# Float64 weights in a planned kernel: a 16-bit copy, a masked shift and one combining pass in place of three VectorE passes

## The chip, the cores and the metric

The kernel runs on one core of a Trainium2 chip. The metric is the device time of one execution in microseconds (us), from its start to its end on that core. The profile covers one such execution. Its span is a little shorter than the execution's time, because launch and completion lie outside it.

## The reference

Four sequences of 768 positions go through windowed attention with 8 heads of 64, and then through a gated feed-forward block. The weights `moe_w_in` (512 x 1024) and `moe_w_out` (512 x 512) reach the kernel as float64, because they are scaled by a float64 number; `moe_w_sg` (768 x 768) is float32.

```python
scores = scale * np.matmul(q, k.transpose(0, 1, 3, 2)) + bias[None, :, :, :]
scores = np.where(keep, scores, -1000000000.0)        # 8 global keys, 96 local ones
a = np.exp(scores - np.max(scores, axis=-1, keepdims=True))
a = a / (np.sum(a, axis=-1, keepdims=True) + 1e-09)
attn = np.matmul(a, v).astype(np.float32)             # then laid out as x [B, S, 512]
...
h = gelu(x @ w_in)
u, v = (h[..., :d_ff // 2], h[..., d_ff // 2:])
v_n = (v - mu) / np.sqrt(var + 1e-06) * g_ln
v_s = np.einsum('ts,bsd->btd', w_sg, v_n) + b_sg[None, :, None]
return (x + (u * v_s) @ w_out).astype(np.float32)
```

## The kernel before

**Attention.** The work is cut into 48 units: a batch, a pair of heads and 256 query rows. Each unit loads its q and k (`qk`) and its `v`, multiplies scores on TensorE (`s_ps`, line 915), adds the bias and takes the row extreme on VectorE (line 937), exponentiates on ScalarE (line 942), adds a tiny number to the sums (`pst`, line 951) and takes their reciprocal (line 955). For the first 16 units the probabilities are turned on TensorE (`tps<-diag,p`, line 1040) against a diagonal matrix that holds the reciprocals (`diag`, line 973, on VectorE or GpSimd). From unit 16 on they are scaled in place (lines 961 and 963) and turned through VectorE and DRAM (`tt`, `far`, `pt`). Then they multiply `v` (`av`, line 1070).

**Feed-forward.** Every fp32 product is made of three matmuls on a high and a low part (lines 577 to 579 in `Moe.terms`; `win`, `wsg` and `wout` hold both parts of the weights). For each batch there are six products of the normalised half (`win,x`), eight of the gate's half (`x,win`), eight of the sequence mix (`wsg,z`) and eight of the output (`gt,wout`). They are laid among the attention units of the next batch.

**Weights.** `load_split` brings one chunk of a weight matrix in: 4 chunks of 512 columns of `w_in` first (the normalised half, staged in the places called z), then 8 of 256 columns (the gate's half, places gt), then 8 of 256 columns of `w_out` (places t and diag). These 20 are float64, so a chunk arrives as pairs of 32-bit words, `raw`, the low word first. ScalarE multiplies the high word, read as a float32, by 2^-112 into `f` (line 742). Three VectorE passes follow: shift `f` left by 3 (line 745), OR in the low word's top three bits (line 747), OR in the high word's sign (line 749). After that `f` is an fp32 number; it is rounded to the high part (752 on ScalarE or 753 on VectorE), and the rest becomes the low part (754 on GpSimd or VectorE). Chunks of `w_sg` need only these last two.

**What sets the order.** A planner (`Plan`) gets every operation with its possible engines, each with a time that the code states (`on_act`, `on_dve`, `on_pool` and so on), and its reads and writes. It draws 200 plans from a fixed seed, each with its own random shifts of the due times, replays each, and keeps the best. The instructions are issued in that order, and each engine runs its own in that order. In gaps that the planner foresees on TensorE in the first 29 us, `keep_on` puts matmuls that multiply zeros (line 526, called fillers here) so that the engine isn't idle there; their results are overwritten.

Of the kernel before, what the change touches and what calls it, by code (L numbers as in the profile page):

```python
# [13 lines left out]
F32R = mybir.dt.float32r  # L14
BF16 = mybir.dt.bfloat16
I32 = mybir.dt.int32
AF = mybir.ActivationFunctionType
ALU = mybir.AluOpType
PSUM = bass.MemoryType.PSUM
# [101 lines left out]
def on_act(n, more=0.0):  # L121

    return "ACT", 0.055 + n / 1200 + more, 0.165 + n / 1200 + more


def on_dve(n, more=0.0):
    return "DVE", 0.065 + n / 960 + more, 0.155 + n / 960 + more


def on_dve_sb(n, more=0.0):  # L130

    return "DVE_SB", 0.065 + n / 960 + more, 0.155 + n / 960 + more


def on_pool(n, more=0.0):
    return "POOL", 0.05 + n / 390 + more, 0.08 + n / 390 + more


def on_pool_ts(n, more=0.0):

    return "POOL_TS", 0.05 + n / 390 + more, 0.08 + n / 390 + more
# [36 lines left out]
def parts(used):  # L178

    return [(b.buf, b.part) if isinstance(b, View) else b if isinstance(b, tuple) else (b, None)  # L180
            for b in used]
# [35 lines left out]
class Now:  # L217
# [5 lines left out]
    def op(self, ways, reads=(), writes=()):  # L223
        for b, _ in parts(writes):
            if b.kind and b.tile is None:
                n = self.next[b.kind] = self.next.get(b.kind, -1) + 1
                b.slot = n % self.places[b.kind]
        ways[0][-1]()
# [325 lines left out]
class Moe:  # L554
# [38 lines left out]
    def gelu2(self, out, h, n):  # L593

        nc, op = self.nc, self.plan.op
        op([on_act(n) + (lambda: nc.scalar.activation(
            out.ap, h.ap, AF.Square, scale=math.sqrt(GELU_C * GELU_A)),)], [h], [out])
        op([on_dve(n) + (lambda: nc.vector.scalar_tensor_tensor(
            out.ap, out.ap, GELU_C, h.ap, ALU.add, ALU.mult),)], [h], [out])
        op([on_act(n, 0.05) + (lambda: nc.scalar.activation(out.ap, out.ap, AF.Tanh),)], [], [out])  # L600
        op([on_dve(n) + (lambda: nc.vector.scalar_tensor_tensor(
# [125 lines left out]
def load_split(nc, plan, stage, t, src, k, cols, part):  # L727


    n, op = cols.stop - cols.start, plan.op  # L730
    rows = slice(k * P, (k + 1) * P)
    wire = lambda words: ("SP", 0.38, P * words * 4 / RATE)
    raw, f = stage(n)
    if src.dtype != mybir.dt.int64:
        op([wire(n) + (lambda: nc.sync.dma_start(f.ap, src[rows, cols]),)], [], [f])
    else:
        words = lambda: raw.ap.bitcast(I32).rearrange("p (n w) -> p n w", w=2)
        a = lambda: f.ap.bitcast(I32)
        op([wire(2 * n) + (lambda: nc.sync.dma_start(
            raw.ap.bitcast(I32), src.bitcast(I32)[rows, 2 * cols.start:2 * cols.stop]),)], [], [raw, f])  # L740

        op([on_act(n, 0.07) + (lambda: nc.scalar.mul(
            f.ap, words()[:, :, 1].bitcast(F32), 2.0 ** -112),)], [raw], [f])

        op([("DVE_SB", 0.07 + n / 1850, 0.15 + n / 1850, lambda: nc.vector.tensor_scalar(
            a(), a(), 3, None, ALU.logical_shift_left))], [], [f])
        op([on_dve_sb(n, 0.02) + (lambda: nc.vector.scalar_tensor_tensor(  # L747
            a(), words()[:, :, 0], 29, a(), ALU.logical_shift_right, ALU.bitwise_or),)], [raw], [f])
        op([on_dve_sb(n, 0.02) + (lambda: nc.vector.scalar_tensor_tensor(  # L749
            a(), words()[:, :, 1], -0x80000000, a(), ALU.bitwise_and, ALU.bitwise_or),)],  # L750
           [raw], [f])
    op([on_act(n, 0.03) + (lambda: nc.scalar.copy(t[:, 0, k, cols], f.ap),),
        on_dve_sb(n / 2) + (lambda: nc.vector.tensor_copy(t[:, 0, k, cols], f.ap),)], [f], [(t, part)])
    lo = lambda eng: eng.tensor_tensor(t[:, 1, k, cols], f.ap, t[:, 0, k, cols].bitcast(F32),  # L754
                                       ALU.subtract)
    op([on_pool(n) + (lambda: lo(nc.gpsimd),), on_dve_sb(n) + (lambda: lo(nc.vector),)],
       [f], [(t, part)])


def local_global_attention_moe(tc, qk_in, v_in, q_t, k_t, v_n, n_gl, w_in, g_ln, w_sg_t, b_sg,  # L760
# [11 lines left out]

    nc.scalar.activation(small[:, 1:2], w.mhalf, AF.Exp)

# [21 lines left out]

    ni = cp.tile([P, 4], I32, name="ni")
    nc.sync.dma_start(ni, n_gl.bitcast(I32).rearrange("(o n) -> o n", o=1).to_broadcast([P, 4]))

# [125 lines left out]
    def softmax(n):  # L925
# [4 lines left out]
        for i in range(2):  # L930
            own = u == 0 and i == 0
            for g in range(2):
# [9 lines left out]
                op([on_act(nk, 0.225) + (lambda p=p, g=g, nk=nk, i=i: nc.scalar.activation(  # L942
                    p[:, g, 0:nk], p[:, g, 0:nk], AF.Exp, bias=st[:, 0, i, g:g + 1], scale=-1.0,
                    accum_out=st[:, 1, i, g:g + 1]),)], [], [(p, g), (st, (i, g))])

        def sums(a):
            return st.ap.rearrange("p a i g -> p a (i g)")[:, a]

        op([on_act(4, 0.13) + (lambda: nc.scalar.activation(
            sums(1), sums(1), AF.Identity, bias=w.tiny),),  # L950
            ("POOL_TS", 0.24, 0.28, lambda: nc.gpsimd.tensor_scalar(  # L951
# [316 lines left out]
    def phase(ns, items, prep=()):  # L1268

        total = sum(c for c, _ in items)  # L1270
        items, prep, done = list(items), list(prep), 0

        def upto(part):
            nonlocal done
            while items and done + items[0][0] / 2 <= part * total:
                c, f = items.pop(0)
                done += c
                f()

        n_prep, todo = len(prep), []  # L1280
        while len(ns) and (todo[-1][-1] if todo else ns[0] - 1) < ns[-1]:
            todo.append(group(todo[-1][-1] + 1 if todo else ns[0]))
        for a, group_ns in enumerate(todo):
            step(group_ns)
            while prep and n_prep - len(prep) < (a + 1) * n_prep / len(todo):
                load_split(nc, plan, *prep.pop(0))
            upto((a + 1) / len(todo))
        upto(2)
# [33 lines left out]
    for b in range(B + 1):  # L1322
# [30 lines left out]
        if b == 1:  # L1353
            general = cp.tile([P, 1], I32, name="general")
            op([("DVE", 0.9, 1.0, find_general)], [xs[b, 0, 0]], [])
# [11 lines left out]
def dense_path(tc, future, ng, nl, iota, w, qkv, out):  # L1367
    nc = tc.nc
    q_t, k_t, v_n = qkv
    with ExitStack() as ctx:  # L1370
# [20 lines left out]
        with tc.For_i(0, B, 1) as b:  # L1391
            x = []
            for j in range(NPAIR):
# [10 lines left out]
                for i in range(NT):  # L1404
# [6 lines left out]
                    for h in range(2):  # L1411
# [16 lines left out]
                        nc.vector.tensor_scalar(s, s, st[:, 0:1], None, ALU.subtract)  # L1428
                        nc.scalar.activation(s, s, AF.Exp, accum_out=st[:, 1:2])
                        nc.vector.tensor_scalar(st[:, 1:2], st[:, 1:2], 1e-9, None, ALU.add)  # L1430
# [79 lines left out]
```

## Time and profile before

| | |
|---|---|
| Time, median of 3 runs | 417.9 us (415.46 to 419.92) |
| Profiled execution | 416.7 us |
| Its span | 414.8 us |
| TensorE busy | 402.6 us (97%) |
| VectorE busy | 309.8 us (75%) |
| ScalarE busy | 223.1 us (54%) |
| GpSimd busy | 202.6 us (49%) |

In rows of the profile PE is TensorE, DVE is VectorE, ACT is ScalarE, POOL is GpSimd and SP is the queue that issues the DMAs; `L749` is line 749 of the kernel. A row such as `stage<-stage 128x256` names the tile that is written, the tiles that are read, and the shape; the staging tiles of the weights, `raw` and `f` alike, are called `stage`. "Idle before" is the time for which the engine stood still ahead of an instruction, and the name behind it is what ended that time. "Issue" means that the engine waited for nothing that the profile shows.

### The profile page before, as it was taken

The numbers are of one execution on the slowest core, as the hardware profiler recorded it, in microseconds if no ns is written. First come the engines' busy times: TensorE is split into PE (matmuls) and PEld (weight loads), VectorE is DVE, ScalarE is ACT, GpSimd is POOL, SyncE is SP. The second block draws the span as 40 slices with busy tenths as digits, with TensorE's granted clock in tenths as the row PEclk, the third lists the DMA queues.
The fourth block names the chain that finished last, engine by engine and source line by source line (L and its number), as shares of the span: only waits on it lengthen the run. The fifth ranks groups of instructions, "written<-read, shape, count | busy, mean of one in ns | idle before, by whom it ended". The sixth has DMA issues, their size and how long they took to land.

```text
span 414.8 us, 12362 instructions
## 1 busy us (share of the span) xinstructions
PE 402.6 (97%) x4579; PEld 363.2 (88%) x4580; DVE 309.8 (75%) x1014; ACT 223.1 (54%) x731; POOL 202.6 (49%) x340
## 2 busy tenths in 40 slices
PE   8899989999999999999999999999999999999994
PEld 5677767899998888999999888999999888999994
DVE  6898889999977888966666798956767568743362
ACT  5988997966747565654155665644245234311220
POOL 2324546677868666654455277354355342323200
PEclk9999999999999999999999999999999999999998
DMA  7856583438889686754697685645777501001002
GB/s 234 298 170 202 185 269 107 141 131 241 256 263 299 203 252 202 207 141 135 191 295 222 188 276 145 193 107 160 218 227 205 171 33 40 0 2 57 21 2 81
DMA packets 50034, 70.21 MB, mean 169 GB/s; under 512 B 5808, under 2 KB 33968, under 8 KB 49968
## 3 DMA queue, kind: packets, MB, share of 16 engines
q1 hardware_dynamic: 49968, 69.36, 55.7%
q8 instruction: 38, 0.62, 0.6%
q14 instruction: 28, 0.23, 0.2%
HBM read 50.99 MB, written 18.35 MB: 167 GB/s over the span
## 4 chain that ended last, share of the span: by engine, by line
PE 86%; DVE 4%; ACT 3%; DMA 2%; issue 2%; POOL 1%; SPq 1%; POOLq 0%; DVEq 0%; ACTq 0%
PE mm_ps L577 24%; PE mm_ps L579 22%; PE mm_ps L578 22%; PE av L1070 7%; PE s_ps L915 7%; PE tps L1040 2%; ACT p L942 2%; DMA pt<-far 1%; DMA stage<-in_w_in_dram 1%; PE s_ps L526 1%; DVE p L937 1%; DVE stage L747 1%; DVE stage L749 1%; SPq L1013 1%; POOL z L615 0%
## 5 line engine op out<-in xcount | busy, mean ns | idle before, releaser
L942 ACT ACTIVATE p<-p,pst 128x192 f32<-128x192 f32 (+1 forms) x192 | 84.2, 443 | 43.4 <-DVE pst L937 43.2
L577 PE MATMUL mm_ps<-wsg,z 128*128 128x384 f32 x192 | 64.7, 337 | 0.0
L579 PE MATMUL mm_ps<-wsg,z 128*128 128x384 f32 x192 | 64.3, 335 | 0.2 <-POOL z L615 0.2
L578 PE MATMUL mm_ps<-wsg,z 128*128 128x384 f32 x192 | 64.2, 334 | 0.0
L963 POOL TENSOR_SCALAR p<-p,pst 128x192 f32<-128x192 f32 (+1 forms) x124 | 56.7, 473 | 14.0 <-DVE pst L955 11.1
L937 DVE CUSTOM_DVE_ANT_0 p<-s_ps,bias 128x192 f32<-128x192 f32 (+1 forms) x192 | 56.6, 339 | 5.7 <-PE s_ps L915 5.5
L1070 PE MATMUL av<-pt,v 64*64 64x128 f32 (+1 forms) x1408 | 48.1, 250 | 2.5 <-issue 1.8
L1070 PEld LDWEIGHTS av<-pt,v 64*64 64x64 f32 x1408 | 40.9, 133 | 10.7 <-issue 6.7
L703 POOL TENSOR_TENSOR o<-o,x 128x384 f32<-128x384 f32 x28 | 28.4, 1013 | 38.3 <-DVE o L700 27.7
L577 PE MATMUL mm_ps<-x,win 128*128 128x384 f32 x128 | 44.1, 344 | 0.0
L915 PE MATMUL s_ps<-qk 64*64 64x192 f32 (+1 forms) x768 | 41.9, 323 | 1.7 <-issue 1.7
L579 PE MATMUL mm_ps<-x,win 128*128 128x384 f32 x128 | 42.9, 335 | 0.6 <-POOL win L754 0.6
L577 PE MATMUL mm_ps<-gt,wout 128*128 128x384 f32 x128 | 43.0, 336 | 0.0
L579 PE MATMUL mm_ps<-gt,wout 128*128 128x384 f32 x128 | 43.0, 336 | 0.0
L578 PE MATMUL mm_ps<-gt,wout 128*128 128x384 f32 x128 | 42.8, 335 | 0.0
L578 PE MATMUL mm_ps<-x,win 128*128 128x384 f32 x128 | 42.8, 334 | 0.0
L577 PE MATMUL mm_ps<-win,x 128*128 128x512 f32 x96 | 40.0, 417 | 0.0
L1005 DVE STREAM_TRANSPOSE tt<-p 128x384 f32<-128x384 f32 (+1 forms) x64 | 33.5, 545 | 7.3 <-DMA far<-tt 5.5
L578 PE MATMUL mm_ps<-win,x 128*128 128x512 f32 x96 | 37.7, 392 | 0.0
L579 PE MATMUL mm_ps<-win,x 128*128 128x512 f32 x96 | 37.6, 392 | 0.0
L951 POOL TENSOR_SCALAR pst<-pst 128x4 f32<-128x4 f32 x45 | 12.3, 273 | 50.6 <-ACT p L942 47.1
L942 ACT ACTIVATION_READ_ACCUMULATOR p<-p,pst 128x1 f32 x192 | 37.0, 193 | 0.0
(106 smaller groups left out, 901.4 us busy)
## 6 DMA issues: line engine op xcount, KB each, us to landing
qk<-in_qk_in_dram SPq DMA_DIRECT2D x32, 416.0 KB, 4.4
far<-tt SPq DMA_DIRECT2D x96, 96.0 KB, 2.6
pt<-far SPq DMA_DIRECT2D x24, 384.0 KB, 4.2
v<-in_v_in_dram SPq DMA_DIRECT2D x32, 256.0 KB, 3.7
out_dram<-o SPq DMA_DIRECT2D x32, 192.0 KB, 2.8
qk<-in_qk_in_dram SPq DMA_DIRECT2D x16, 288.0 KB, 3.6
v<-in_v_in_dram SPq DMA_DIRECT2D x16, 192.0 KB, 4.3
far<-tt SPq DMA_DIRECT2D x32, 80.0 KB, 2.8
```

Of the source, the lines that this page charges most:

```text
L577: mm(ps.ap, ah, bh, start=(i == 0), stop=False)
L578: mm(ps.ap, ah, bl, start=False, stop=False)
L579: mm(ps.ap, al, bh, start=False, stop=(i == n - 1))
L703: lo = lambda eng: eng.tensor_tensor(o.ap, o.ap, xm[:, 1, :].bitcast(F32), ALU.add)
L915: nc.tensor.matmul(to, qk[rows, qc:qc + HQ], keys, start=True, stop=True)
L937: nc.vector.tensor_tensor_reduce(out=p[:, g, 0:nk], in0=s_ps[h][:, i * W:i * W + nk], in1=bias[:, 2 * j + h, w0:w0 + nk], op0=ALU.add, op1 ...
L942: op([on_act(nk, 0.225) + (lambda p=p, g=g, nk=nk, i=i: nc.scalar.activation(p[:, g, 0:nk], p[:, g, 0:nk], AF.Exp, bias=st[:, 0, i, g:g + ...
L951: ("POOL_TS", 0.24, 0.28, lambda: nc.gpsimd.tensor_scalar(sums(1), sums(1), 1e-9, None, ALU.add)),
L963: op([on_pool_ts(nk, -0.10) + (partial(scaled, lambda o, a, c: nc.gpsimd.tensor_scalar(o, a, c, 1.0, ALU.mult, ALU.mult)),), on_act(nk, 0. ...
L1005: nc.vector.transpose(out, src.rearrange("p g (b j) -> p g b j", j=QB))
L1040: nc.tensor.matmul(tps[r][g * HQ:(g + 1) * HQ, a * HQ:(a + 1) * HQ], pc[rows, c:c + HQ], diag[rows, 2 * i + c // W], start=True, stop=True)
L1070: nc.tensor.matmul(to, v[rows, vc:vc + D], of, stop=True, skip_group_check=True, **kw)
```

## The change

The sign and the three low bits of the result now come from one word. The top half of the low word (16 bits) is copied over the bottom half of the high word, which ScalarE has read by then. So the high word holds the sign at the top and the three wanted bits at places 15 to 13. An arithmetic shift right by 13 brings those to the bottom and leaves the sign at the top, and a mask with 0x80000007 clears the rest. One pass then shifts `f` left by 3 and ORs this word in.

```diff
-        op([("DVE_SB", 0.07 + n / 1850, 0.15 + n / 1850, lambda: nc.vector.tensor_scalar(
-            a(), a(), 3, None, ALU.logical_shift_left))], [], [f])
-        op([on_dve_sb(n, 0.02) + (lambda: nc.vector.scalar_tensor_tensor(
-            a(), words()[:, :, 0], 29, a(), ALU.logical_shift_right, ALU.bitwise_or),)], [raw], [f])
-        op([on_dve_sb(n, 0.02) + (lambda: nc.vector.scalar_tensor_tensor(
-            a(), words()[:, :, 1], -0x80000000, a(), ALU.bitwise_and, ALU.bitwise_or),)],
-           [raw], [f])
+        halves = lambda: raw.ap.bitcast(U16).rearrange("p (n w) -> p n w", w=4)
+        beside = lambda eng: eng.tensor_copy(halves()[:, :, 2], halves()[:, :, 1])
+        op([on_pool_ts(n) + (lambda: beside(nc.gpsimd),),
+            ("DVE_SB", 0.07 + n / 1850, 0.15 + n / 1850, lambda: beside(nc.vector))], [], [raw])
+        op([("DVE_SB", 0.07 + n / 1850, 0.15 + n / 1850, lambda: nc.vector.tensor_scalar(
+            words()[:, :, 1], words()[:, :, 1], 13, -0x7FFFFFF9, ALU.arith_shift_right,
+            ALU.bitwise_and))], [], [raw])
+        op([on_dve_sb(n, 0.02) + (lambda: nc.vector.scalar_tensor_tensor(
+            a(), a(), 3, words()[:, :, 1], ALU.logical_shift_left, ALU.bitwise_or),)], [raw], [f])
```

The line numbers of the changed kernel are larger by 1 ahead of this place and by 5 behind it; the copy is its line 749, the masked shift 752, the combining pass 755. The planner gives the copy to GpSimd for 13 chunks (12 of 256 columns and one of 512) and to VectorE for 7 (4 of 256 and three of 512). The number of operations is the same, but their engines, times and dependences are not, and the search ends at another plan for the whole kernel. Three places show it.

The first place is VectorE's order late in the loading of the first four chunks. `pst` with a reciprocal and `diag` belong to the sixth unit, whose diagonal matrix is built here. Before:

```order
L749 SCALAR_TENSOR_TENSOR stage<-stage 128x512 x2
L745 TENSOR_SCALAR stage<-stage 128x512
L747 SCALAR_TENSOR_TENSOR stage<-stage 128x512
L955 RECIPROCAL pst<-pst 128x4
L749 SCALAR_TENSOR_TENSOR stage<-stage 128x512
L973 TENSOR_TENSOR diag<-ident_h,pst 128x256
L753 CAST win<-stage 128x512
```

With the change:

```order
L960 RECIPROCAL pst<-pst 128x4
L759 TENSOR_TENSOR win<-stage,win 128x512
L978 TENSOR_TENSOR diag<-ident_h,pst 128x256
L749 COPY stage<-stage 128x512
L752 TENSOR_SCALAR stage<-stage 128x512
L755 SCALAR_TENSOR_TENSOR stage<-stage 128x512
L1191 TENSOR_TENSOR x<-xh,x 128x256
```

The passes of the fourth chunk stood ahead of the sixth unit's diagonal matrix, and now stand behind it.

The second place is TensorE's order at the first feed-forward product, where fillers (`mm_ps<-bsg`) stand ahead of the first matmul on weights. Before:

```order
L1070 MATMUL av<-pt,v 64x128 x4
L526 LDWEIGHTS bsg
L526 MATMUL mm_ps<-bsg 128x512
L526 LDWEIGHTS bsg
L526 MATMUL mm_ps<-bsg 128x512
L526 LDWEIGHTS bsg
L526 MATMUL mm_ps<-bsg 128x512
L577 MATMUL mm_ps<-win,x 128x512
```

With the change:

```order
L1075 MATMUL av<-pt,v 64x128 x4
L527 LDWEIGHTS bsg
L527 MATMUL mm_ps<-bsg 128x512
L578 MATMUL mm_ps<-win,x 128x512
L579 MATMUL mm_ps<-win,x 128x512
```

Three fillers became one here. Over the whole start there were 12 of 384 columns, 28 of 320, 10 of 128, 15 of 384 and 3 of 512, and there are now 12 of 384, 30 of 320, 6 of 128, 16 of 384 and 1 of 512. The first 12 of 384 and then 19 (now 20) of 320 stand ahead of the first turning.

The third place is GpSimd's order where the chunks of 256 columns come in (`rs` is a statistic of the normalisation, `wsg` and `win` are the low parts of weights). Before:

```order
L973 TENSOR_TENSOR diag<-ident_h,pst 128x256
L951 TENSOR_SCALAR pst<-pst 128x4
L640 TENSOR_TENSOR rs<-rs,small 128x1
L754 TENSOR_TENSOR wsg<-stage,wsg 128x384 x2
L951 TENSOR_SCALAR pst<-pst 128x4 x2
L754 TENSOR_TENSOR win<-stage,win 128x256 x3
```

With the change:

```order
L749 COPY stage<-stage 128x256
L978 TENSOR_TENSOR diag<-ident_h,pst 128x256
L749 COPY stage<-stage 128x256
L1191 TENSOR_TENSOR x<-xh,x 128x256
L641 TENSOR_TENSOR rs<-rs,small 128x1
L956 TENSOR_SCALAR pst<-pst 128x4
L749 COPY stage<-stage 128x256 x2
L759 TENSOR_TENSOR win<-stage,win 128x256
L759 TENSOR_TENSOR wsg<-stage,wsg 128x384 x3
```

Four copies now stand ahead of the first low part on GpSimd, and two of the three low parts of `win` have gone from it to VectorE, which has 5 of them now and had 3. In the whole order VectorE also takes 3 low parts of `wout` from GpSimd, and gives it 2 of `wsg`.

More of the change, by code (lines that the diff above doesn't have):

```diff
@@ L16 @@
 I32 = mybir.dt.int32
+U16 = mybir.dt.uint16
 AF = mybir.ActivationFunctionType
```

## The prediction

> **What bounds the kernel now.** I read the page's busy shares first, and then the stretches of the span.
>
> ```profile
> span 414.8 us, 12362 instructions
> PE 402.6 (97%) x4579; PEld 363.2 (88%) x4580; DVE 309.8 (75%) x1014; ACT 223.1 (54%) x731; POOL 202.6 (49%) x340
> ```
>
> TensorE is busy for 97%, so VectorE's time can count only where TensorE stands still or burns time. The windows view gives each engine's busy time by stretch; I cut it where the fillers end (30.4 us), where TensorE becomes continuous (86 us), and where the last weights are in.
>
> ```profile
> core 0: us, PE busy (x) PEld busy (x) DVE busy (x) ACT busy (x) POOL busy (x), PEclk, DMA share, GB/s
> 0.00:10.10 10.10, 8.60 (x65) 4.92 (x65) 6.43 (x34) 5.41 (x19) 2.91 (x19) 1.00 0.73 233
> 10.10:30.40 20.30, 17.80 (x517) 13.76 (x518) 18.12 (x65) 18.25 (x67) 5.32 (x9) 1.00 0.72 240
> 30.40:60.00 29.60, 29.60 (x778) 23.45 (x778) 26.16 (x118) 28.16 (x109) 13.03 (x25) 1.00 0.70 221
> 60.00:86.00 26.00, 23.45 (x269) 19.32 (x262) 23.99 (x83) 22.50 (x74) 17.34 (x22) 1.00 0.38 121
> 86.00:115.00 29.00, 29.00 (x270) 27.77 (x271) 28.16 (x76) 17.72 (x54) 23.78 (x33) 1.00 0.75 219
> 115.00:400.00 285.00, 284.61 (x2650) 264.74 (x2642) 200.89 (x632) 130.54 (x412) 140.26 (x234) 1.00 0.55 162
> 400.00:414.80 14.80, 9.53 (x55) 9.21 (x54) 6.05 (x12) 0.51 (x1) 0.00 (x0) 0.93 0.16 58
> ```
>
> From 86 to 400 us TensorE stands still for 0.39 us. What VectorE saves there buys nothing, and the tail (14.80 - 9.53 = 5.27 us) has no weights in it. What can be had lies in two stretches: 20.30 - 17.80 = 2.50 us idle up to 30.4 us, and 26.00 - 23.45 = 2.55 us between 60 and 86. The same view for line 526 alone (TensorE and its weight loads) shows what of the busy time is filler.
>
> ```profile
> 0.00:10.10 10.10, 6.78 (x31) 3.43 (x31) 1.00 0.73 233
> 10.10:30.40 20.30, 5.52 (x36) 2.79 (x37) 1.00 0.72 240
> ```
>
> So 5.52 us of the 17.80 carry nothing, and 8.0 of the 20.3 us are not work. TensorE's list of waits says what ended its idle time.
>
> ```profile
> PE av L1070 <- issue: 1.8, 2, 1.3
> PE s_ps L915 <- issue: 1.7, 1, 1.7
> PE mm_ps L579 <- POOL win L754: 0.6, 1, 0.6
> PE av L1070 <- ACT pt L1048: 0.3, 1, 0.3
> PE tps L1040 <- DVE diag L973: 0.2, 1, 0.2
> ```
>
> Of 4.6 us here, 3.5 are "issue", which no engine's work ends. Weights end one wait (0.6 us), VectorE another (0.2 us). That second one shows the weights' part in the start; it stands in the chain that ended last, here in order of time (start, duration, what):
>
> ```profile
> 23.70 1.43 DVE stage L749 x2
> 25.13 0.25 issue
> 25.38 0.42 DVE stage L745
> 25.83 0.69 DVE stage L747
> 26.61 0.64 DVE stage L749
> 27.25 0.35 DVE diag L973
> 27.73 0.93 PE tps L1040 x48
> ```
>
> For 3.5 us the sixth unit's diagonal matrix stands behind passes over weights, and TensorE fills that time with zeros.
>
> **The change part by part.** Durations come from the groups by shape (busy us, mean ns):
>
> ```profile
> L745 DVE TENSOR_SCALAR stage<-stage 128x256 int32<-128x256 int32 x16 | 5.4, 344 | 0.0
> L747 DVE SCALAR_TENSOR_TENSOR stage<-stage 128x256 int32<-128x256 int32 x16 | 6.5, 426 | 0.2
> L749 DVE SCALAR_TENSOR_TENSOR stage<-stage 128x256 int32<-128x256 int32 x16 | 7.5, 495 | 0.0
> L745 DVE TENSOR_SCALAR stage<-stage 128x512 int32<-128x512 int32 x4 | 1.7, 418 | 0.1
> L747 DVE SCALAR_TENSOR_TENSOR stage<-stage 128x512 int32<-128x512 int32 x4 | 3.2, 798 | 0.1
> L749 DVE SCALAR_TENSOR_TENSOR stage<-stage 128x512 int32<-128x512 int32 x4 | 3.2, 820 | 0.0
> L754 DVE TENSOR_TENSOR win<-stage,win 128x512 fp32r<-128x512 f32 x4 | 2.7, 684 | 0.0
> ```
>
> *VectorE.* The three passes cost 27.5 us in all. The combining pass reads two tensors as line 747 does, with every second word in one: 6.5 + 3.2 us. The masked shift has one source as line 745 has, but reads and writes every second word. Line 745 is its lower end (344 and 418 ns) and line 747, at one element a step, its upper one (426 and 798). I take the lower one, for in this trace a hop of one word cost nothing on the read side: line 747 took 0.69 us in the chain above, the contiguous line 754 684 ns. The seven copies have the same ends, and I take the lower: 3 x 418 + 4 x 344 ns = 2.6 us. So VectorE has 9.7 + 7.1 + 2.6 = 19.4 us, 8.1 less. Of these, 4 x 820 - 3 x 418 ns = 2.0 us lie in the first stretch; the rest lies behind 60 us, beside TensorE work.
>
> [...]
>
> *GpSimd* gets 13 copies. No row has a copy, so these bound it:
>
> ```profile
> L963 POOL TENSOR_SCALAR p<-p,pst 128x192 f32<-128x192 f32 x108 | 50.8, 485 | 12.3 <-DVE pst L955 9.4 <-DMA v<-in_v_in_dram 2.4 <-PE av L1070 0.4
> L963 POOL TENSOR_SCALAR p<-p,pst 128x128 f32<-128x128 f32 x16 | 6.2, 394 | 1.7 <-DVE pst L955 1.7
> L754 POOL TENSOR_TENSOR wout<-stage,wout 128x256 fp32r<-128x256 f32 x8 | 6.7, 833 | 1.8 <-DVE stage L749 0.6 <-DVE y L672 0.6 <-DVE u L601 0.5
> L754 POOL TENSOR_TENSOR wsg<-stage,wsg 128x384 fp32r<-128x384 f32 x4 | 4.0, 1012 | 7.9 <-ACT wsg L752 3.5 <-DVE wsg L753 2.4 <-ACT xh L1168 2.0
> ```
>
> Line 963 adds 91 ns for 64 elements, which makes 576 ns at 256; the two-source line 754 takes 833. A one-source copy is nearer to the first. I take 0.65 us, in all 12 x 0.65 = 7.8 us behind 60 us. From 60 to 115 us GpSimd is busy for 17.34 + 23.78 = 41.1 of 55 us and hands five low parts to VectorE (5 x 0.83 = 4.2 us) for two of 384 columns. It holds the copies beside its other work.
>
> *The added wait.* In 13 chunks VectorE's masked shift now waits for GpSimd, and everything behind it in VectorE's order waits with it: softmax passes for the scores, and the normalisation that TensorE's mix products need. Against the old chain of a chunk (344 + 426 + 495 ns at 256 columns) the new one is 650 + 344 + 426: 0.16 us longer plus a hand-over, on each chunk. The planner puts shifts of several chunks together, so the first one's delay is mostly all that shows. I count 0 and keep -0.6 (the wait for line 754 at GpSimd gone) and +0.7 (as much again, should a chunk come late). Line 742 reads the word ahead of the copy, as it did ahead of line 745, so nothing new waits on ScalarE. The DMAs keep their number; a place in gt still comes free when the low part is made.
>
> *Fillers.* In the first stretch their columns go from 11456 to 10624. The 36 recorded hold 10944 columns in 5.52 us, 0.50 ns each: -0.42 us. One more of 320 columns stands ahead of it: +0.16. Fillers are executed whether VectorE is early or not, so the 2.0 us that VectorE saves become time only as far as fillers were left out or a wait goes: here -0.26 us.
>
> *The sixth unit's diagonal matrix* no longer waits for the fourth chunk: the 0.2 us go. Next late there is ScalarE, busy for 18.25 of 20.30 us and not relieved, which is why I count no more.
>
> *Issue.* These waits may move with the instruction count; I count 0 and keep -3.5 and +1.8 (one more of the longest).
>
> Sum: 416.7 - 0.26 - 0.2 = 416.2 us against the profiled execution. That execution is 1.2 us below the median of the runs shown, so the same step from the median gives 417.4. I forecast the middle, 416.8 us.
>
> **The rivals.** *TensorE's start closes up.* All the waits go that can: 3.5 of issue and 1.1 of the others, with 0.26 of filler: 411.8 us. For it speaks that VectorE was on the chain; against it, that issue isn't VectorE's and that the planner left nearly as many fillers. Half of it gives 414, which I leave to the fringe of the forecast.
>
> *GpSimd becomes the bound.* From 60 to 115 us it has 55 - 41.1 = 13.9 us free, plus 4.2 - 2.0 handed over (a low part of 384 taken at 1 us): 16.1 us. Twelve copies fill that at 1.34 us each. At 1.8 us, over twice line 754's 833 ns, they are 5.5 us too long, the shifts on VectorE (52.2 of 55 us busy) and the mix products behind them come late by that, and the kernel takes 416.2 + 5.5 = 421.7 us by the profile, 422.9 by the median. Against it: line 963 does arithmetic at 485 ns for 192. For it: 16-bit elements with gaps are in no row.
>
> *Every second word written is slow.* At the upper ends the seven passes of 512 columns in the first stretch take 7 x 0.38 = 2.7 us more. They eat the 2.0 us saved, and on a chain that TensorE follows: 418.9 us. [...]
>
> *The copies don't relieve VectorE at all:* only if the planner gave most to VectorE. It gave 7 of 20, so I leave that out.
>
> **How the numbers follow.** The forecast has 0.63, with 414.5 to 418.5 as its own range; the start closing up 0.12, GpSimd as the bound 0.13, slow writes 0.12. The range reaches from halfway into the first rival (413.2) to most of the way to the second (420.8), which leaves 1 in 10 on each side. One per cent is 4.2 us, about what a measurement can tell from no change. Faster by more (below 413.7) is the first rival alone: 0.12. Slower by more (above 422.1) is the second: 0.12, the last hundredth being one that stays within. The same: 0.76.
>
> **What would show it.** In the profile of the changed kernel the masked shift should take about 344 and 418 ns, the combining pass 426 and 798, the copy on GpSimd 0.58 to 0.83 us at 256 columns, and VectorE's staging work 19 to 20 us. TensorE should stay continuous from about 86 us on, with line 527 at about 5.1 us between 10 and 30 us, and a wait for `diag` gone. The prediction is wrong if copies on GpSimd take over 1.3 us, if TensorE waits for `win`, `z` or `wout` behind 60 us for more than 2 us in all, or if the issue waits change by more than 2 us.

## The result and the profile after

| | before | after |
|---|---|---|
| median of 19 runs each | 416.21 us (413.14 to 419.92) | 418.61 us (417.85 to 419.57) |
| after to before | | 1.0051, 95% interval 1.0034 to 1.0068 |
| span of the profiled execution | 414.8 us | 416.6 us |

The kernel became slower by half a per cent. That is within the one per cent that the prediction called the same, and the time lies in the range, but the forecast had a small gain (416.2 against 416.7 us) and the interval lies wholly on the other side of 1. The two profiled executions differ by 1.8 us, near the 2.4 us of the medians, so the profile can be asked where they are. It is one execution of each, and those of the kernel before differ among themselves by more than that, so it can point at places and not prove them.

The head of the page and the stretches, cut at the same times as before (columns: stretch, its length, busy time of PE, PEld, DVE, ACT and POOL, granted clock, DMA share, GB/s):

```profile
span 416.6 us, 12379 instructions
PE 403.3 (97%) x4577; PEld 363.1 (87%) x4577; DVE 305.2 (73%) x1001; ACT 216.8 (52%) x718; POOL 222.4 (53%) x366
```

```profile
0.00:10.10 10.10, 8.73 (x64) 5.03 (x64) 6.30 (x34) 5.21 (x18) 2.90 (x19) 1.00 0.73 234
10.10:30.40 20.30, 18.04 (x517) 14.02 (x516) 18.60 (x70) 17.51 (x64) 7.08 (x11) 1.00 0.76 240
30.40:60.00 29.60, 27.60 (x711) 21.82 (x710) 24.34 (x106) 27.21 (x106) 15.04 (x29) 1.00 0.68 212
60.00:86.00 26.00, 24.24 (x322) 19.81 (x320) 25.52 (x79) 21.18 (x66) 18.77 (x25) 1.00 0.42 128
86.00:115.00 29.00, 28.37 (x232) 26.51 (x229) 26.58 (x77) 18.40 (x60) 22.41 (x31) 1.00 0.76 225
115.00:400.00 285.00, 285.00 (x2680) 264.95 (x2680) 197.24 (x629) 126.21 (x409) 153.85 (x251) 1.00 0.55 161
400.00:416.60 16.60, 11.29 (x66) 10.97 (x64) 6.61 (x12) 1.03 (x2) 2.35 (x2) 1.00 0.15 52
```

Length less busy time is TensorE's idle time:

| stretch, us | idle before | idle after | difference |
|---|---|---|---|
| 0 to 30.4 | 4.00 | 3.63 | -0.37 |
| 30.4 to 60 | 0 | 2.00 | +2.00 |
| 60 to 86 | 2.55 | 1.76 | -0.79 |
| 86 to 115 | 0 | 0.63 | +0.63 |
| 115 to 400 | 0.39 | 0 | -0.39 |
| 400 to the end | 5.27 | 5.31 | +0.04 |

That is 1.1 us more idle time, and TensorE is busy for 0.7 us more: together the 1.8 us. VectorE did get relief (305.2 instead of 309.8 us), and GpSimd has 20 us more. All of the additional idle time is there by 54 us (5.1 us against 4.0 before), and by then GpSimd has made one of its 13 copies, at 16.97 us; the others start at 55.11 us or later. Behind 54 us, where they run, TensorE's idle time is what it was before. TensorE's waits from 30.4 to 60 us, then from 60 to 86, then from 86 to 115 (engine, line, who ended the wait: us in total, times, longest):

```profile
PE tps L1045 <- DVE x L1187: 1.1, 1, 1.1
PE tps L1045 <- issue: 0.5, 1, 0.5
PE tps L1045 <- POOL diag L978: 0.4, 1, 0.4
```

```profile
PE mm_ps L580 <- DVE z L616: 0.7, 1, 0.7
PE s_ps L920 <- DVE pst L942: 0.4, 1, 0.4
PE mm_ps L580 <- DVE win L759: 0.3, 1, 0.3
PE tps L1045 <- DVE diag L978: 0.2, 1, 0.2
```

```profile
PE mm_ps L580 <- DVE wout L759: 0.6, 1, 0.6
```

The issue waits fell from 3.5 to 0.5 us, and more than that came back as waits that VectorE and GpSimd end. The longest is at the turning of the seventh unit. The chain that ended last shows what stood ahead of it on VectorE (start, duration, what):

```profile
27.16 0.41 DVE diag L978
27.57 0.67 DVE stage L749
...
28.27 0.44 DVE stage L752
...
28.73 0.69 DVE stage L755
...
30.31 0.60 DVE win L759
...
33.19 0.22 DVE x L1187
33.41 0.96 PE tps L1045 x48
```

The fourth chunk's three passes, which were moved from ahead of the sixth unit's diagonal matrix to behind it, now stand ahead of the seventh unit's. But VectorE is not later there than before: the seventh unit's matrix starts at 32.57 us, and before at 32.68. What differs is the work that TensorE has ahead of the turning. Before (the first of three matmuls on `win`, and the turning) and with the change:

```profile
32.67 0.50 PE L577 MATMUL mm_ps<-win,x 128*128 128x512 f32 x1
33.56 0.93 PE L1040 MATMUL tps<-diag,p 64*64 64x64 f32 x48
```

```profile
33.41 0.93 PE L1045 MATMUL tps<-diag,p 64*64 64x64 f32 x48 [1.13 <-DVE x L1187]
```

The turning begins 0.15 us earlier than before. Three matmuls that filled the time ahead of it now stand behind it, and two fillers less stand ahead of the first product, so TensorE comes to the turning early and waits. So this wait belongs to the new order; that VectorE's passes or GpSimd's copies cause it isn't shown.

The sixth unit's matrix gained nothing: it starts at 27.16 us, and before at 27.17. The 0.2 us of idle time ahead of its turning are gone, but two more fillers stand there (10 of 384 columns instead of 8), and the turning begins at 27.72 us instead of 27.73. What came last for it is now another low part of the weights: VectorE's row of line 759 started at 26.36 us and took 0.88.

The groups of the staging work:

```profile
L749 POOL COPY stage<-stage 128x256 uint16<-128x256 uint16 x12 | 9.9, 838 | 1.4 <-POOL wout L759 0.8 <-ACT stage L743 0.4
L755 DVE SCALAR_TENSOR_TENSOR stage<-stage 128x256 int32<-128x256 int32 x16 | 7.1, 462 | 0.3
L752 DVE TENSOR_SCALAR stage<-stage 128x256 int32<-128x256 int32 x16 | 5.4, 345 | 0.1
L755 DVE SCALAR_TENSOR_TENSOR stage<-stage 128x512 int32<-128x512 int32 x4 | 2.8, 690 | 0.0
L749 DVE COPY stage<-stage 128x256 uint16<-128x256 uint16 x4 | 2.3, 575 | 0.0
L749 DVE COPY stage<-stage 128x512 uint16<-128x512 uint16 x3 | 2.2, 743 | 0.0
L752 DVE TENSOR_SCALAR stage<-stage 128x512 int32<-128x512 int32 x4 | 1.8, 470 | 0.1
```

VectorE's part is 21.6 us (27.5 before, 19.4 forecast). The means hide one thing, which the order in time shows. Two rows of one masked shift of 256 columns, the first beside a copy on GpSimd, the second with GpSimd idle:

```profile
79.95 0.95 POOL L749 COPY stage<-stage 128x256 uint16<-128x256 uint16 x1
80.17 0.88 DVE L752 TENSOR_SCALAR stage<-stage 128x256 int32<-128x256 int32 x1
83.11 0.28 DVE L752 TENSOR_SCALAR stage<-stage 128x256 int32<-128x256 int32 x1
```

The first took three times as long and ended with the copy, 0.15 us behind it. A rounding to `win` beside the one copy of 512 columns does much the same:

```profile
16.97 1.36 POOL L749 COPY stage<-stage 128x512 uint16<-128x512 uint16 x1 [0.73 <-ACT stage L743]
17.16 1.45 DVE L758 CAST win<-stage 128x512 fp32r<-128x512 f32 x1
```

The same rounding took 0.42 us in the kernel before, with GpSimd idle:

```profile
27.50 0.42 DVE L753 CAST win<-stage 128x512 fp32r<-128x512 f32 x1
```

Behind the slow rounding VectorE made the fourth unit's diagonal matrix, which ended at 18.93 us; the turning that needs it began at 19.08, after 0.38 us of idle time of TensorE (which the profile puts down to ScalarE's line 743). A product of two tensors was held up too. Beside the copies from 59.53 to 61.37 us this one took 0.73 us, and 0.40 to 0.43 with GpSimd idle, and TensorE waited 0.2 us for it:

```profile
60.68 0.73 DVE L978 TENSOR_TENSOR diag<-ident_h,pst 128x256 f32<-128x256 bf16 x1
```

### The profile page after: what moved, and what is told of

Its sections match the earlier page's. It is cut to its first block, busy times and chain, and to the rows that moved or that the text cites. A ratio compares the mean times of both kernels' runs of the same rounds, so it can differ in the third digit from the quotient of the medians.

```text
span 416.6 us, 12379 instructions
## 1 busy us (share of the span) xinstructions
PE 403.3 (97%) x4577; PEld 363.1 (87%) x4577; DVE 305.2 (73%) x1001; ACT 216.8 (52%) x718; POOL 222.4 (53%) x366
## 4 chain that ended last, share of the span: by engine, by line
PE 75%; DVE 16%; ACT 4%; issue 2%; DMA 1%; POOL 0%; SPq 0%; ACTq 0%; POOLq 0%; DVEq 0%
PE mm_ps L578 21%; PE mm_ps L580 20%; PE mm_ps L579 20%; PE s_ps L920 6%; PE av L1075 6%; ACT p L947 3%; DVE p L942 2%; DVE stage L755 2%; DVE stage L752 1%; DMA qk<-in_qk_in_dram 1%; DVE stage L749 1%; DVE vg L643 1%; DVE win L759 1%; PE tps L527 1%; PE tps L1045 1%
## 5 line engine op out<-in xcount | busy, mean ns | idle before, releaser
L1075 PE MATMUL av<-pt,v 64*64 64x128 f32 (+1 forms) x1408 | 47.2, 250 | 0.5 <-PE av L1075 0.5
L580 PEld LDWEIGHTS mm_ps<-wsg,z 128*128 128x128 f32 x192 | 36.0, 188 | 1.3 <-DVE z L616 1.3
```

What stands on the lines that cost most here:

```text
L580: mm(ps.ap, al, bh, start=False, stop=(i == n - 1))
L1075: nc.tensor.matmul(to, v[rows, vc:vc + D], of, stop=True, skip_group_check=True, **kw)
```

## The experiments

Four explanations stood against each other at first. **The passes:** the new passes themselves save less than priced. **The wait:** VectorE waits for GpSimd's copies, and what is queued behind it comes late. **The plan:** the search simply drew a worse plan of its 200, or the old one was a lucky one. **The price:** the planner gives VectorE's copy 0.07 us and n/1850, too little, and plans on that. The fifth, **the hold-up** of VectorE's fast passes by a copy on GpSimd, was formed on the first runs. The expectations number the theories in their own way and say in brackets what each means. All ratios are to the kernel before on the same chip, with 95% intervals.

**The passes alone.** The planner is shown the operations of before, so that its order on VectorE stays as it was, and in the three places stand the copy (on VectorE), the masked shift and the combining pass. The added lines alone:

```diff
+        op([("DVE_SB", 0.07 + n / 1850, 0.15 + n / 1850, lambda: beside(nc.vector))], [], [f])
+        op([on_dve_sb(n, 0.02) + (lambda: nc.vector.tensor_scalar(words()[:, :, 1], words()[:, :, 1],
+            13, -0x7FFFFFF9, ALU.arith_shift_right, ALU.bitwise_and),)], [raw], [f])
+        op([on_dve_sb(n, 0.02) + (lambda: nc.vector.scalar_tensor_tensor(a(), a(), 3,
+            words()[:, :, 1], ALU.logical_shift_left, ALU.bitwise_or),)], [raw], [f])
```

> The planner is shown the operations of before, so every engine keeps the order of before; in the places of the three old passes stand the 16-bit copy (on VectorE), the masked shift and the combining pass. Theory 1 (the copy on VectorE costs as much as the pass that it replaces: 743 against 418 and 575 against 344 ns, while the shift costs 470 against 798 and 345 against 426): VectorE's staging work stays within 2 us of the 27.5 us of before, and the time within 1 us of before (415.5 to 417.2). Theory 2 (only the other plan made the time): the same time as before too, 416.2. Theory 3 (the new passes are faster on VectorE, by the price that the planner used): 1 to 2 us below before.

Measured: 0.9996 (0.9958 to 1.0035). Its groups:

```profile
L747 DVE COPY stage<-stage 128x256 uint16<-128x256 uint16 x16 | 8.1, 519 | 0.2
L752 DVE SCALAR_TENSOR_TENSOR stage<-stage 128x256 int32<-128x256 int32 x16 | 7.4, 486 | 0.0
L749 DVE TENSOR_SCALAR stage<-stage 128x256 int32<-128x256 int32 x16 | 4.6, 307 | 0.2
L752 DVE SCALAR_TENSOR_TENSOR stage<-stage 128x512 int32<-128x512 int32 x4 | 3.2, 818 | 0.0
L747 DVE COPY stage<-stage 128x512 uint16<-128x512 uint16 x4 | 3.0, 738 | 0.2 <-ACT stage L743 0.2
L749 DVE TENSOR_SCALAR stage<-stage 128x512 int32<-128x512 int32 x4 | 2.2, 542 | 0.1
```

They make 28.5 us, against 27.5 before. Three passes are still three passes: VectorE's copies take 11.1 us, as much as the dearest of the old passes (10.7 us), and only a copy that leaves VectorE saves anything there. Nothing is lost either.

**The wait.** The same, with every copy on GpSimd (`beside(nc.gpsimd)` in the first line).

> The order of before again, with the copy on GpSimd at the place in the order where the first pass stood. VectorE's staging work falls to about 18 us (20 shifts and 20 combining passes). Theory 1 (VectorE's work in the start sets the time): below before by 0.5 to 1.5 us. Theory 2: within 0.5 us of before. Theory 4 (shifts that wait for GpSimd's copies, 0.84 us at 256 columns and 1.36 at 512, hold up VectorE's order, and that is what the change lost): 2 us or more above before, with idle time of VectorE ahead of the masked shifts.

Measured: 1.0128 (1.0081 to 1.0175), 422.92 us. The wait at VectorE's masked shift (line 749 here), and the groups of GpSimd's copies:

```profile
DVE stage L749 <- POOL stage L747: 11.1, 9, 3.1
```

```profile
L747 POOL COPY stage<-stage 128x256 uint16<-128x256 uint16 x16 | 12.7, 821 | 2.7 <-PE av L1073 2.5
L747 POOL COPY stage<-stage 128x512 uint16<-128x512 uint16 x4 | 6.0, 1498 | 2.2 <-PE av L1073 1.1 <-ACT stage L743 1.1
```

VectorE stands still for 11.1 us in nine places, the longest 3.1 us. In an order that wasn't made for them, copies on GpSimd cost 1.3%.

**The copies without the wait.** As in the first run, and beside each copy on VectorE GpSimd makes 16-bit copies of 256 elements from the bias table to a tile that nobody reads (one for a chunk of 256, two for 512). This is work in addition; nobody waits for it. The added lines alone:

```diff
+            *(nc.gpsimd.tensor_copy(plan.scratch, plan.source.rearrange(
+                "p (n w) -> p n w", w=4)[:, 0:256, 1]) for _ in range(n // 256)),
```

> The kernel of the run with the order of before and all copies on VectorE, and beside each copy one that GpSimd makes of 256 16-bit elements with the same gaps (two for a chunk of 512) from the bias table into a scratch tile that nobody reads. GpSimd does the work of the run with its copies in that order (ratio 1.0128), but nothing on VectorE waits for it. Theory 5a (the waits for GpSimd's copy are the cost; VectorE stood still for 11.1 us ahead of the shifts there): within 0.3% of before. Theory 5b (GpSimd's copies cost by what they do to others: they hold up VectorE's fast passes beside them, 0.88 for 0.28 us and 1.45 for 0.42 us in the changed kernel, and delay GpSimd's own work): 0.8% or more above before.

Measured: 1.0069 (1.0036 to 1.0101). The groups:

```profile
L749 POOL COPY scratch<-bias 128x256 uint16<-128x256 uint16 x24 | 13.1, 547 | 4.8 <-PE av L1078 4.3
L747 DVE COPY stage<-stage 128x256 uint16<-128x256 uint16 x16 | 9.0, 577 | 0.1
L755 DVE SCALAR_TENSOR_TENSOR stage<-stage 128x256 int32<-128x256 int32 x16 | 8.5, 555 | 0.0
```

Copies for which nobody waits cost 0.7%, some half of the run before, with 13.1 us of GpSimd's time instead of 18.7. That is more than theory 5a allows and a little less than the 0.8% that 5b had set. In the same order VectorE's copy is at 577 instead of 519 ns and the combining pass at 555 instead of 486, and TensorE waits for low parts that GpSimd makes:

```profile
PE mm_ps L580 <- POOL wout L760: 1.1, 2, 0.5
PE mm_ps L580 <- POOL win L760: 0.7, 1, 0.7
PE mm_ps L580 <- POOL z L616: 0.6, 1, 0.6
```

So the copies on GpSimd had two costs here that are no wait for a copy: VectorE's passes took longer (577 for 519 ns, 555 for 486), and GpSimd's own low parts came late for TensorE (the waits above, 2.4 us in all, which the first run doesn't list). The intervals of the two runs overlap, so the half is rough, and this run doesn't split the two costs.

**The plan.** Another seed for the search, for the kernel before and for the changed one.

```diff
-        rnd = random.Random(1)
+        rnd = random.Random(2)
```

> The kernel before with another seed for the planner's random draws, and nothing else. Theory 2b (the plan of before is a lucky draw that the change gave up; the passes themselves are worth next to nothing): 0.3 to 0.8% slower than before, as the three plans of the changed kernel measured so far (ratios 1.005 to 1.0065). Theory 5 (the change costs about 0.5% whatever the plan, for instance by the copies on GpSimd): within 0.2% of before.

> A third seed for the kernel before, to see how far apart its plans lie. Theory 2b: 0.3 to 0.8% slower than before. Theory 5: within 0.2% of before.

> The changed kernel with another seed for the planner's random draws, and nothing else. Theory 1: as the changed kernel, 418.6 within 0.5 us, since the prices are the same. Theory 2: another plan and another time, anywhere from 414.5 to 419.5.

> A third seed for the changed kernel. Theory 2b: anywhere from 0 to 0.8% above before, and its three seeds have the same mean as the three seeds of before within 0.3%. Theory 5: 0.4 to 0.7% above before, like its other two seeds.

Measured: before with seeds 2 and 3 is at 1.0005 (0.9972 to 1.0037) and 1.0000 (0.997 to 1.003); the changed kernel at 1.0054 (1.0022 to 1.0085) and 1.0076 (1.004 to 1.0113), with 8 and 11 copies on GpSimd. Three draws of before lie within 0.05%, three of after all 0.5 to 0.8% above. The plan's luck falls as the cause.

**The price.** VectorE's copy is declared to the planner at 0.065 us and n/960, 0.60 us for 512 columns.

```diff
-            ("DVE_SB", 0.07 + n / 1850, 0.15 + n / 1850, lambda: beside(nc.vector))], [], [raw])
+            on_dve_sb(n) + (lambda: beside(nc.vector),)], [], [raw])
```

> The changed kernel with one number changed: the planner is told that the copy on VectorE takes as long as a full-rate pass (0.60 us at 512 columns, not 0.35). Theory 1 (the plan came out worse because this price was half of what the copy takes): back to the time of before or below, 415 to 416.5 us. Theory 2 (it is a matter of which plan is drawn): another draw, anywhere from 414.5 to 419.

Measured: 1.0065 (1.003 to 1.01), with 9 copies on GpSimd. This price alone is not the cause. If, beside that price, GpSimd is no longer offered the copy, all 20 stay on VectorE:

> The changed kernel with the copy allowed on VectorE alone, at its measured length in the planner (a full-rate pass); GpSimd copies nothing and no shift waits for it. With the order of before, these passes measured 0.9996 of before. Theory 5 (copies on GpSimd are the cost): within 0.2% of before. Theory 2b: another draw, 0.3 to 0.8% above before.

Measured: 0.9992 (0.9967 to 1.0017). So a plan made for the new passes is level with before as soon as no copy is on GpSimd, in line with the first run.

**The hold-up.** The planner knows two kinds of work on GpSimd. Beside one (`on_pool`) it places none of VectorE's fast or two-source passes, and it adds an order between the two engines. The other (`on_pool_ts`) it takes to be free of that. The change declares the copy as the second kind. Here it is the first, and VectorE's copy has the price above:

```diff
-        op([on_pool_ts(n) + (lambda: beside(nc.gpsimd),),
+        op([on_pool(n) + (lambda: beside(nc.gpsimd),),
```

> The changed kernel with the copy on VectorE at its measured length in the planner, and the copy on GpSimd declared as one that VectorE's fast passes can't run beside, as the planner does for GpSimd's two-source operations. Theory 5b: the planner keeps fast passes away from the copies or leaves them to VectorE; within 0.2% of before. Theory 5a: as with the true price alone, 0.4% or more above before, as long as GpSimd still gets half of the copies.

> The changed kernel with both prices corrected (VectorE's copy at a full-rate pass, GpSimd's copy as one that VectorE's fast passes can't run beside) and another seed. If the wrong belief on GpSimd's copies made most of the loss: 1.000 to 1.003 of before, as with the first seed. If GpSimd's copies cost in any plan, and 1.0023 was a lucky draw: 1.005 to 1.0075.

> The same with a third seed. Wrong belief: 1.000 to 1.003. GpSimd's copies in any plan: 1.005 to 1.0075.

And this edit without the price:

> The changed kernel with GpSimd's copy declared as one that VectorE's fast passes can't run beside, and the old price of the copy on VectorE, which is half of what it takes. Wrong belief on GpSimd alone: 1.000 to 1.003. If the price on VectorE matters as much, or if GpSimd's copies cost in any plan: 1.004 to 1.0075.

| the planner's belief | ratios (seeds 1, 2, 3 where there are several) | copies on GpSimd |
|---|---|---|
| as in the change | 1.0051, 1.0054, 1.0076 | 13, 8, 11 |
| price right, hold-up unknown | 1.0065 (1.003 to 1.01) | 9 |
| hold-up known, price as in the change | 1.003 (0.9997 to 1.0062) | 9 |
| both right | 1.0023 (0.9987 to 1.006), 0.9993 (0.9965 to 1.0022), 0.9952 (0.992 to 0.9983) | 12, 11, 9 |

All four plans that don't know of the hold-up are above all four that do, though single intervals overlap. The mean with both right is 0.9989, of the four at the top 1.0062. The first with both right lies a little over the 0.2% that was expected, the other two below the 1.000 to 1.003. It isn't the number of copies, which overlaps. For each VectorE instruction to 126 us that ran beside a copy I took by how much it was longer than the shortest of its form in any of the runs. Added up, that is 4.6 us in the changed kernel, 2.5 and 3.3 with the other seeds and 2.8 with the price alone; 1.6, 1.2 and 1.3 with both right and 1.1 with the hold-up alone. That these microseconds of VectorE are the loss itself isn't shown. The edit also adds an order between the two engines, and a planner that keeps them apart also places other work otherwise; the runs don't tell these apart.

The third seed is the one version that beats both kernels: 415.47 us against 417.47 for the kernel before on the same chip, its profiled span 411.0 us. It is the best of three draws, and their mean is no gain that can be told from before.

**The copy on ScalarE**, or VectorE where the planner prefers that; none on GpSimd. The added lines alone:

```diff
+        op([on_act(n, 0.07) + (lambda: nc.scalar.copy(halves()[:, :, 2], halves()[:, :, 1]),),
+            on_dve_sb(n) + (lambda: beside(nc.vector),)], [], [raw])
```

> The changed kernel with the copy allowed on ScalarE or VectorE, none on GpSimd. ScalarE is busy for 40 of 55 us behind 60 us, and VectorE for 52. If VectorE's work in the weights' time sets TensorE's waits: 0.2 to 0.5% below before. If not, or if a wait for another engine is what costs (theory 5a): from before to 0.5% above.

Measured: 1.0029 (0.9996 to 1.0062). The copy is dearer there than the float pass over the high word beside it:

```profile
L750 ACT COPY stage<-stage 128x256 uint16<-128x256 uint16 x14 | 10.5, 786 | 0.2
L743 ACT ACTIVATE stage<-stage 128x256 f32<-128x256 f32 x16 | 6.8, 437 | 0.1
```

With 10.5 us and 3 x 1356 ns more on ScalarE, the run can't be told from no change and decides nothing about the hold-up.

## Why the prediction was right or wrong

**What bounds the kernel: right.** What happens from 115 us on made 0.35 us less idle time, and the rest lies ahead of that. But the prediction asked only where time could be saved; the largest new idle time, 2.00 us, lies from 30.4 to 60 us, where before there was none.

**Masked shift and combining pass: right, in the sum.** 5.4 + 1.8 + 7.1 + 2.8 = 17.1 us, 16.8 forecast. The third rival (every second word written is slow) falls for these passes: an undisturbed masked shift of 512 columns (at 28.27 us) took 0.43 us, as the contiguous shift of before did (418 ns).

**VectorE's copy: mis-sized.** The step was "I take the lower", 418 and 344 ns. Measured: 743 and 575 ns, 4.5 us instead of 2.6. Both are nearer to the upper ends that I had named (798 and 426 ns); at 256 columns some of the 575 may be hold-up, since the two runs with all copies on VectorE have 519 and 541. The reason I gave, reads with a hop cost nothing, came from a 32-bit pass (line 747 at 0.69 us, the contiguous line 754 at 684 ns); the copy is of 16-bit elements, which no row showed.

**GpSimd "holds the copies beside its other work": the step that failed.** By busy time it held: 18.77 + 22.41 = 41.2 us from 60 to 115, as much as before (41.1), since low parts went to VectorE; the copy took 838 ns, hardly over the bound of 833, so the second rival, GpSimd as the bound at 1.34 us a copy, didn't come. But free time on GpSimd was taken to be free, and the copies there were counted at nothing. A copy there takes time from VectorE beside it (0.28 to 0.88 us, 0.42 to 1.45 us), and the four plans made without knowing of the hold-up lost 0.5 to 0.8%, where the same passes without copies on GpSimd lost nothing (0.9996 and 0.9992). With unread copies TensorE also waited for low parts that GpSimd makes (1.1, 0.7 and 0.6 us); in the changed kernel's profile no such wait reaches 0.2 us. The trace shows that VectorE was held up, in one-source passes by the rows above and in reads of two tensors by the diagonal matrix (0.73 us for 0.40); by what means isn't shown. I had weighed no rival on it.

**The added wait, counted as 0:** where the planner knew of the copy, the changed kernel shows no such wait among those that count: line 752 has 0.1 us of idle time ahead of 16 passes. Where it didn't know, it was 11.1 us. So the 0 held for this kernel, by the planner's work.

**Sixth unit's diagonal matrix, -0.2, "next late there is ScalarE": wrong on both.** The passes did move behind it, but it came at the same time (27.16 us), and fillers took the place of the 0.2 us. Next late there was VectorE itself, with another low part, and not ScalarE.

**Fillers, -0.26:** recorded are 6.75 + 5.71 us against 6.78 + 5.52, 0.16 us more. About 5.1 us were forecast for the second number.

```profile
0.00:10.10 10.10, 6.75 (x32) 3.48 (x32) 1.00 0.73 234
10.10:30.40 20.30, 5.71 (x35) 2.65 (x33) 1.00 0.76 240
```

**Issue, counted as 0 with -3.5 as one end:** it went by -3.0, close to that end. By the prediction's own test (over 2 us) this is a miss. It bought nothing, since other waits took its place. In the profiles of the other plans these waits make 0 to 4.3 us and don't go with the time: the kernel before with seed 2 has none at 413.4 us of span, the price alone has 4.3 at 417.0, and the fastest plan 1.9 at 411.0. So the first rival (the start closes up, 411.8 us, by way of issue) was priced on a term that is given back.

**TensorE continuous from 86 us on:** nearly; 0.63 us between 86 and 115. **Waits for `win`, `z` and `wout` behind 60 us:** 1.6 us, under the 2 us that I had set as a limit.

The time fell into the range because the forecast's terms were small either way; as far as the account goes, that is luck. The direction was wrong: in place of -0.46 us stands +1.8 in the spans and +2.4 in the medians.

The cause that the runs show is copies on GpSimd under a plan that takes them to be free beside VectorE: without them the loss is gone, with the plan told it is gone in the mean of four plans (1.0000), and unread copies alone bring 0.7%. How they cost remains open. It can be the hold-up itself, later work on GpSimd, or a plan that is worse throughout because it was drawn up on a wrong belief. For the last speaks that in the changed kernel's profile the additional idle time lies ahead of 54 us and so ahead of twelve of the thirteen copies, in good part at a turning that the new order of TensorE leaves waiting; that is one execution, and no run tests it.

## What to carry to other kernels

Price a new pass from a row of its own element type, engine and step between elements; if there is none, take the dearer end until one is measured (VectorE's copy of 512 columns was counted at 418 ns and took 743). Idle time of an engine is not free if its work slows a busier neighbour (here a shift of 0.28 us took 0.88 beside a copy), so look in the order in time for instructions that take two or three times as long as others of their form, and at what runs beside them. Where a planner sets the order, a wrong belief about what may run side by side can cost whatever the seed (here 0.5 to 0.8% under all three); run several seeds of both kernels before calling a plan unlucky, and tell the planner before judging the edit.

## What the runs showed of the hardware

- VectorE copied 16-bit elements that lie 8 bytes apart in 519 ns for 256 and 738 for 512 in the mean of the first run, while its masked shift over 32-bit words that lie 8 bytes apart took 307 ns for 256 in the same run. The narrower type was the slower one.
- ScalarE took 786 ns for the same copy of 256 elements, against 437 for a pass that reads 32-bit floats at the same step and writes them densely (both in the run with the copy on ScalarE).
- GpSimd took 803 to 873 ns for it in place (means of the runs), and 547 ns where the destination is dense (the unread copies). The source is another tile there, so that the destination is the reason isn't shown.
- A masked shift on VectorE that met a copy on GpSimd took 0.88 instead of 0.28 us in the changed kernel and ended 0.15 us behind it; a product of two tensors took 0.73 instead of 0.40.
